# Own PSUM banks for two products of the first down projection, and half of W_out prepared one set earlier

## Chip, cores and metric

The kernel runs on one core of one Trainium2 chip. The metric is the device time of one launch in microseconds (us). Before the change it was 1612.12 us, the median of three runs (1608.09 to 1612.94).

## What is computed

```python
x = attention(q, k, v)              # chunks of 64, 8 heads of 64, 4608 tokens -> 4608 x 512
h = np.maximum(x @ w_in, 0.0)       # up1:   512 -> 2048
y = h * h @ w_out                   # down1: 2048 -> 512
g = y @ w_gate                      # up2:   512 -> 1536, gate and value
a = g * (1 / (1 + exp(-g))) * (y @ w_val)
out = a @ w_out2                    # down2: 1536 -> 512
```

Every large product is exact to float32: a float32 operand is split into a high and a low part, and three matmuls (high by high, weight's low by high, weight's high by low) make one product. The weights come as 64-bit floats that the kernel itself decodes.

## The kernel before, in words

**Tiling.** The 4608 tokens are nine blocks of 512. They are worked on in five sets: `sets[0]` is block 0 alone (a single), `sets[1]` to `sets[4]` are pairs of blocks. For a pair, a 2 x 2 block product is done with seven products in place of eight (Strassen-Winograd); they are numbered 1 to 7, and the weights are kept as a *combo*, a tile `W` with the seven weight combinations, high and low parts. For a product the operands `hi` and `lo` are made by ScalarE (`high`, line 170) and VectorE (`low`, line 173).

**up1.** For each set there are eight jobs, one for each pair of feature blocks (keys 0 to 7); a job is seven products of six matmuls (42 matmuls; the matmuls of every product stand in `three`, lines 551 to 553), in four *quarters*, so that a set has 32 quarters. `beside1` (the function that is called at every quarter `t`) puts other work beside the products: the attention of the next pair, the sums for the next set, and in the last set the preparation of W_out. Keys 0, 3 and 6 of W_in stay in SBUF, the five others move through two slots of the pool `wp` (five slots) and are loaded again by `load_combo` (line 262, `W<-wi`). The products' results leave PSUM as copies on ScalarE (line 641: `r`, `u`) and additions on VectorE (line 627: `g`). The attention of a unit is: scores on PE (406), maximum, subtraction and sums on VectorE, exponential on ScalarE, normalising on POOL (445), a transpose on VectorE (483), a copy on ScalarE (492), four small DMAs `p<-z` on the SP queue (501), and the value products on PE (526).

**W_out's preparation** (class `Prep`, lines 200 to 258). Per block `j` of eight: two raw loads (`raw`, line 115), decoding on ScalarE (142, 143), VectorE (147, 148, 160) and POOL (155), four sums on VectorE (236 to 239), then the high parts on ScalarE and the low parts on VectorE. Blocks 0 to 3 are *resident* (`HELD` = 4): they stay in `wp` slots. Blocks 4 to 7 are `Streamed` (line 269): they are made in two `wp` slots, stored to DRAM (`o`, line 287, two stores each, on POOL's queue) and read back product by product (`ow<-o`, line 1002). All eight are queued in `work` and begun in the last up1 set, set 4, streamed ones first; the raw loads stand on SP's queue, two ahead.

**down1** (class `Down`). For a pair it does products 1, 5, 6, 7, 2, 3, 4, each in four steps of twelve matmuls (48 matmuls a product), each into two PSUM banks, called `acc`. Products 1, 6, 7 and 4 go one after the other onto the same two banks `x`, and the running sums are copied out between them: `kept` (line 1071, ScalarE) takes `r1` after product 1, `u2` after 6, `u3` after 7. Products 5 and 3 go onto `z`, product 2 onto `y`. `put` adds (`add`, line 624, VectorE) and stores the results (1082). A pool of six one-bank buffers (`psb`) serves x, z and y; a buffer of two banks (`psa`) is used by the attention and by up2.

**The order of the work.** Only PE's order is fixed by hand from set 2 on (`tc.manual_schedule` for PE); a scheduler places the instructions on ScalarE, VectorE, POOL and SP, and each of these carries out its own list in that order.

Of the kernel before, what the change touches and what calls it, by code (L numbers as in the profile page):

```python
# [10 lines left out]
F32 = mybir.dt.float32  # L11
# [10 lines left out]
P = 128  # L22
# [7 lines left out]
def attention_mlp_mlp_kernel(  # L30
# [75 lines left out]
    class Raws:  # L106


        def __init__(self, sources, ahead):
            self.sources, self.ahead, self.tiles = list(sources), ahead, []  # L110

        def load(self, n):
# [156 lines left out]
    class Streamed(Prep):  # L269


        stages = {}

        @property
        def w(self):
            k = self.key[1] % 2
            if k not in Streamed.stages:
                w = new_combo().rearrange("p x i c -> p (x i c)")
                Streamed.stages[k] = w.rearrange("p (i x c) -> p x i c", i=7, x=2)
            return Streamed.stages[k]  # L280

        def put(self, roles):
            i, k = divmod(self.key[1], 2)
            if i not in odram:
                odram[i] = dp.tile([P, 7, 2, 2, half], F32, name=f"o{i}")
            w = self.w.bitcast(F32).rearrange("p x i c -> p i x c")
# [613 lines left out]
    early = up1.loads[len(sets) - 1, keys1[5]]  # L900
    up1.loads[len(sets) - 1, keys1[5]] = up1.loads.pop((len(sets) - 1, keys1[4]))

# [64 lines left out]
    class Down:  # L967

        ORDER = ((1,), (5,), (6,), (7,), (2,), (3,), (4,))
        MAKE, LOAD, WEIGHTS = 2, 5, 3

        def __init__(self):
            self.raw, self.ops, self.w = {}, {}, {}
            self.steps = [
                (n, ps, i)
                for n, bs in enumerate(sets)
                for ps in (self.ORDER if len(bs) == 2 else ((1, 5), (2, 4)))
                for i in range(n1 // 2)  # L980
            ]
            self.loaded = self.made = self.weighted = 0
# [11 lines left out]
        def weights(self, upto):  # L994
            while self.weighted < min(upto, len(self.steps)):
                n, ps, i = self.steps[self.weighted]
                self.weighted += 1
                for p in ps:
                    if 2 * i >= HELD:
                        work.until(lambda: ("o", 2 * i + 1) in stored)  # L1000
                        self.w[n, p, i] = big.tile([P, 2, 2, half], F32R, tag="big", name="ow")
                        nc.sync.dma_start(out=self.w[n, p, i].bitcast(F32), in_=odram[i][:, ROLES[p]])
# [41 lines left out]
        def product(self, ps, n, p, i, first, last=True, on=False):  # L1044
            hi, lo = self.ops.pop((n, p, i))
            ws = []
            for k in range(2):
                j = 2 * i + k
                if j < HELD:
                    work.until(lambda: ("o", j) in combos)  # L1050
                    w = [combos["o", j][:, x, ROLES[p]] for x in range(2)]
                else:
                    w = [self.w[n, p, i][:, k, x] for x in range(2)]
                ws.append(w)
            for e in range(2):
                cols = slice(e * P, (e + 1) * P)
                for k, w in enumerate(ws):
                    three(
                        ps[e],
                        (w[0][:, cols], w[1][:, cols]),  # L1060
                        (hi[:, k, :], lo[:, k, :]),
                        first and i == k == 0,
                        last and 2 * i + k == n1 - 1,
                        on,
                    )
# [7 lines left out]

        def put(self, n, i, j, ps, r):
            for e in range(2):
                if r:
                    add(r[e], ps[e], r[e])
                    o = r[e]
                else:
                    o = one("y")  # L1080
                    (nc.vector.tensor_copy if e and len(sets[n]) == 1 else nc.scalar.copy)(out=o, in_=ps[e])
                nc.sync.dma_start(out=ydram[sets[n][j]][1 - i][:, e, :], in_=o)

        def step(self, s):
            n, ps, i = self.steps[s]
            begins, ends = i == 0, i == n1 // 2 - 1

# [18 lines left out]
            elif begins and p == 2:  # L1106
                self.y = two()
            fresh = p in (1, 5, 2)
            self.product(self.z if p in (5, 3) else self.y if p == 2 else self.x, n, p, i, fresh, True, not fresh)
            if not ends:  # L1110
# [162 lines left out]
    HELD = n1 // 2  # L1273
    stored = set()
    down1, down2 = Down(), Last()
# [24 lines left out]
    def beside1(n, m):  # L1300
        def at_quarter(i):
            t = 4 * m + i
            attention_step(n + 1, t)
            attention_step(n + 2, t - LAST)
            if n + 1 < len(sets):
                if t == 24:
                    x_sums(n + 1)
                if t - LAST in OPS:
                    up1.ops[n + 1].make(*OPS[t - LAST])
            else:  # L1310
                work.step(OUT_STEPS[t])
                if t == 17:
                    load_combo(early)
                if t == LAST - 8:
# [6 lines left out]

    def note(j):
        stored.add(("o", j))
        return
        yield

    OUT_STEPS = [1 if t < 4 else 0 if t < 6 else 3 if t % 3 else 2 for t in range(LAST)]

    attention_step(3, -3)
    with ordered(ET.PE):  # L1330
        for n in range(2, len(sets)):
            if n + 1 == len(sets):
                order = [*range(HELD, n1), *range(HELD)]
                raws = Raws([w_out[j + n1 * t] for j in order for t in range(2)], 2)
                made = {j: (Prep if j < HELD else Streamed)(("o", j), raws, j < HELD, False, by_columns) for j in order}
                for j in order:
                    work.add(made[j].steps())
                    work.add(note(j))
            for m in range(n1):
# [251 lines left out]
```

## Time and profile before

| | |
|---|---|
| median of three runs | 1612.12 us |
| the profiled execution, its own time | 1610.74 us |
| its span, first to last instruction | 1608.9 us |
| PE busy | 1557.7 us (97%) |
| VectorE, ScalarE, POOL busy | 1172.7, 819.0, 160.4 us |
| DMA, mean over the span | 241 GB/s |

The span is 1.8 us shorter than the time of the same execution. PE's share of busy time is high all through, so what can be saved is the time between matmuls, and it is read by stage: set 3 of up1 runs from about 281 to 366 us, set 4 (the last) to about 460, down1 from there to about 813, up2 and down2 after that.

### The profile page before, as it was taken

The page shows a single profiled execution, that of the slowest core. Times are in us where ns is not written, and L with a number is a line of the kernel's source. Part 1 is how long each engine was busy: PE and PEld are TensorE (multiplying, and loading weights), DVE is VectorE, ACT ScalarE, POOL GpSimd, SP SyncE. Part 2 cuts the span into 40 slices and gives each one's busy share as a digit, 9 for nine tenths or more (in the row PEclk, how much of TensorE's full clock was granted, in tenths as well). Part 3 has the DMA queues.
Part 4 walks back from the last instruction along what each step waited for, and adds up shares of the span by engine and source line. Part 5 has one row for each costly group of instructions (what it writes and reads, how often), then busy time and mean ns, then how long its engine had stood idle before and what let it go on. Part 6 is the DMA issues. An engine that isn't in the chain of part 4 may idle for free.

```text
span 1608.9 us, 23565 instructions
## 1 busy us (share of the span) xinstructions
PE 1557.7 (97%) x9216; PEld 1279.8 (80%) x9216; DVE 1172.7 (73%) x1392; ACT 819.0 (51%) x1137; POOL 160.4 (10%) x126
## 2 busy tenths in 40 slices
PE   5999999999889999999999999999999999999998
PEld 4788778888668887888788878888888887888886
DVE  7897555657797888998856667457458986887794
ACT  4777666668664544454454444334335644443441
POOL 3122120303300000011001010000000210000000
PEclk9999999999999999999999999999999999999999
DMA  8566786768986887787654644761666999464342
GB/s 315 198 240 216 262 312 222 266 225 287 419 305 232 310 294 272 269 324 274 213 216 186 230 160 157 248 230 53 239 239 237 401 377 407 159 209 146 103 131 53
DMA packets 143679, 387.41 MB, mean 241 GB/s; under 512 B 48465, under 2 KB 57681, under 8 KB 136273
## 3 DMA queue, kind: packets, MB, share of 16 engines
q1 hardware_dynamic: 123600, 327.19, 57.3%
q10 hardware_dynamic: 14592, 38.80, 6.4%
q0 software_dynamic: 5376, 19.92, 3.6%
q8 instruction: 72, 1.18, 0.3%
q14 instruction: 39, 0.31, 0.1%
HBM read 251.92 MB, written 130.81 MB: 238 GB/s over the span
## 4 chain that ended last, share of the span: by engine, by line
PE 89%; DMA 4%; DVE 4%; issue 2%; ACT 1%; POOL 1%; SPq 0%; POOLq 0%; DVEq 0%; ACTq 0%
PE px L551 11%; PE px L553 11%; PE px L552 11%; PE acc L551 7%; PE acc L552 7%; PE acc L553 7%; PE py L551 6%; PE pz L551 6%; PE pz L553 5%; PE pz L552 5%; PE py L553 5%; PE py L552 5%; PE xps L526 1%; DMA raw<-in_w_out_dram 1%; PE s L406 1%
## 5 line engine op out<-in xcount | busy, mean ns | idle before, releaser
L551 PE MATMUL px<-hi,W 128*128 128x512 f32 x640 | 252.1, 394 | 5.6 <-DMA W<-wi 4.0
L553 PE MATMUL px<-lo,W 128*128 128x512 f32 x640 | 249.7, 390 | 0.0
L552 PE MATMUL px<-hi,W 128*128 128x512 f32 x640 | 249.7, 390 | 0.0
L170 ACT CAST hi<-graw 128x1024 fp32r<-128x1024 f32 x124 | 128.1, 1051 | 136.3 <-PE acc L553 39.9
L155 POOL TENSOR_TENSOR m<-m,raw 128x512 int32<-128x512 int32 x68 | 100.9, 1504 | 953.2 <-ACT raw L143 342.3
L641 ACT COPY u<-px 128x512 f32<-128x512 f32 x160 | 92.7, 580 | 156.8 <-PE px L553 149.0
L551 PEld LDWEIGHTS px<-hi,W 128*128 128x128 f32 x640 | 120.4, 188 | 34.8 <-DMA W<-wi 5.0
L170 ACT CAST hi<-h 128x1024 fp32r<-128x1024 f32 x93 | 95.7, 1053 | 96.8 <-DVE h L1181 14.6
L553 PEld LDWEIGHTS px<-lo,W 128*128 128x128 f32 x640 | 120.4, 188 | 25.5
L552 PEld LDWEIGHTS px<-hi,W 128*128 128x128 f32 x640 | 120.4, 188 | 24.4
L551 PE MATMUL pz<-hi,W 128*128 128x512 f32 x320 | 126.3, 395 | 7.1 <-DVE g L627 6.8
L551 PE MATMUL py<-hi,W 128*128 128x512 f32 x320 | 126.3, 395 | 1.1 <-ACT g L786 1.1
L173 DVE TENSOR_TENSOR lo<-graw,hi 128x1024 fp32r<-128x1024 f32 x88 | 109.1, 1248 | 24.8 <-PE acc L552 12.4
L552 PE MATMUL pz<-hi,W 128*128 128x512 f32 x320 | 125.5, 392 | 0.0
L553 PE MATMUL pz<-lo,W 128*128 128x512 f32 x320 | 125.3, 392 | 0.0
L553 PE MATMUL py<-lo,W 128*128 128x512 f32 x320 | 124.9, 390 | 0.0
L552 PE MATMUL py<-hi,W 128*128 128x512 f32 x320 | 124.8, 390 | 0.0
L793 DVE TENSOR_TENSOR g<-g,sig 128x1024 f32<-128x1024 f32 x54 | 65.8, 1220 | 71.8 <-ACT sig L792 71.6
L173 DVE TENSOR_TENSOR lo<-h,hi 128x1024 fp32r<-128x1024 f32 x93 | 110.3, 1211 | 5.4 <-issue 2.2
L551 PE MATMUL acc<-hi,W 128*128 128x512 f32 x256 | 101.0, 394 | 6.0 <-ACT r L1071 5.1
L552 PE MATMUL acc<-hi,W 128*128 128x512 f32 x256 | 100.3, 392 | 0.5 <-DVE W L173 0.5
L551 PE MATMUL acc<-hi,ow 128*128 128x512 f32 x256 | 99.6, 389 | 0.0
(130 smaller groups left out, 3296.3 us busy)
## 6 DMA issues: line engine op xcount, KB each, us to landing
g<-g ACTq DMA_DIRECT2D x72, 512.0 KB, 5.4
graw<-g SPq DMA_DIRECT2D x72, 512.0 KB, 5.6
ow<-o SPq DMA_DIRECT2D x64, 512.0 KB, 5.0
W<-wv SPq DMA_DIRECT2D x16, 1792.0 KB, 8.2
h<-g SPq DMA_DIRECT2D x54, 512.0 KB, 6.6
h<-h SPq DMA_DIRECT2D x54, 512.0 KB, 5.8
W<-wg SPq DMA_DIRECT2D x12, 1792.0 KB, 8.4
W<-wi SPq DMA_DIRECT2D x9, 1792.0 KB, 11.8
```

What stands on the lines that cost most here:

```text
L155: nc.gpsimd.tensor_tensor(out=mi[t], in0=mi[t], in1=halves(word(raw, 0, I32)), op=ALU.add)
L170: nc.scalar.copy(out=hi, in_=src)
L173: nc.vector.tensor_tensor(out=lo, in0=src, in1=hi, op=ALU.subtract)
L406: nc.tensor.matmul(out=s[c * CH:(c + 1) * CH, j, (n * pairs + a) * CH:(n * pairs + a + 1) * CH], lhsT=qt[part, n, cols], rhs=kk[part, n, c ...
L526: nc.tensor.matmul(out=xps[c][j * CH:(j + 1) * CH, (a * 2 + n) * CH:(a * 2 + n + 1) * CH], lhsT=vt[part, n, h * CH:(h + 1) * CH], rhs=rhs, ...
L551: nc.tensor.matmul(out=ps, lhsT=lh, rhs=rh, start=first, stop=False, skip_group_check=on)
L552: nc.tensor.matmul(out=ps, lhsT=ll, rhs=rh, start=False, stop=False, skip_group_check=on)
L553: nc.tensor.matmul(out=ps, lhsT=lh, rhs=rl, start=False, stop=last, skip_group_check=on)
L641: nc.scalar.copy(out=r, in_=self.x)
L793: nc.vector.tensor_tensor(out=g[j], in0=g[j], in1=s, op=ALU.mult)
```

## The change

Two things, which share no code but the order of the blocks.

*Down1's banks.* Product 7 opens two banks of its own (`x7`, the two-bank buffer of `psa`) rather than going on in `x`, and product 4 goes on in them. The sum `u3` is then product 7's banks plus `u2`, two additions on VectorE (`sum_of`) where ScalarE made two copies; after product 4 `put` adds `u2` (two additions on VectorE) where ScalarE made two copies; product 3's result goes to tiles of its own, since `u2` lives on.

*W_out.* The streamed blocks 4 to 7 begin at quarters -30, -21, -11 and -2, counted from the start of set 4, that is from set 3 on, at fixed quarters. Their parts are made in four tiles `os` of the pool `big`, not in `wp` slots, and each is stored by a DMA on ScalarE's queue a quarter later. The resident blocks follow at fixed quarters of set 4. Raw loads stand on POOL's queue, six quarters ahead for streamed blocks, four or five for resident ones. The key order of set 4 becomes 0, 3, 1, 2, 6, 4, 5, 7, with the reloads of keys 4, 5 and 7 tied to the jobs of 3, 1 and 2. The single of down1 takes its feature blocks in the order 2, 3, 0, 1 (the streamed ones first). `make(3)` brings one operand's split forward to quarter 2 of each set.

```diff
         def load(self, n):
             while n > 0 and self.sources:
                 raw = big.tile([P, BLOCK], I64, tag="big", name="raw")
-                nc.sync.dma_start(out=raw, in_=self.sources.pop(0))
+                self.queue.dma_start(out=raw, in_=self.sources.pop(0))
...
     class Streamed(Prep):
-        def put(self, roles):
...
-            nc.gpsimd.dma_start(out=odram[i][:, roles, k], in_=w[:, roles])
-        def l(self):
-            super().l()
-            self.put(slice(0, 3))
-        def n(self):
-            super().n()
-            self.put(slice(3, 7))
+        def stage(self, first, src):
+            w, n = big.tile([P, 2, 2, half], F32R, tag="big", name="os"), src.shape[1]
+            parts_of(src, w[:, :n, 0, :], w[:, :n, 1, :])
             i, k = divmod(self.key[1], 2)
             if i not in odram:
                 odram[i] = dp.tile([P, 7, 2, 2, half], F32, name=f"o{i}")
+            self.put = lambda: nc.scalar.dma_start(out=odram[i][:, first:first + n, k], in_=w.bitcast(F32)[:, :n])
+        def t(self):
+            self.stage(0, self.direct()[:, 0:2, :])
+        def u(self):
+            self.stage(2, self.direct()[:, 2:3, :])
+        def v(self):
+            self.stage(3, self.s[:, 0:2, :])
+        def w(self):
+            self.stage(5, self.s[:, 2:4, :])
...
-    order1[-1] = [keys1[m] for m in (6, 3, 7, 5, 0, 4, 2, 1)]
+    order1[-1] = [keys1[m] for m in (0, 3, 1, 2, 6, 4, 5, 7)]
...
+    for m, after in ((3, 4), (1, 5), (2, 7)):
+        up1.loads[len(sets) - 1, keys1[m]] = keys1[after]
+    up1.loads.pop((len(sets) - 1, keys1[4]))
...
+        SINGLE = (2, 3, 0, 1)
...
+            elif begins and p == 7:
+                x = banks2("x7")
+                self.x7 = [x[:, e, :] for e in range(2)]
-            fresh = p in (1, 5, 2)
+            fresh = p in (1, 5, 2, 7)
+            ps = {5: self.z, 3: self.z, 2: self.y, 7: self.x7, 4: self.x7}.get(p, self.x)
...
             elif p == 7:
-                self.put(n, 1, 1, self.z, self.kept(self.x))
+                self.put(n, 1, 1, self.z, self.sum_of(self.x7, self.u2, "u3"))
             elif p == 2:
                 self.put(n, 0, 0, self.y, self.r1)
             elif p == 3:
-                self.put(n, 0, 1, self.z, self.u2)
+                self.put(n, 0, 1, self.z, self.u2, [one("y"), one("y")])
             elif p == 4:
-                self.put(n, 1, 0, self.x, None)
+                self.put(n, 1, 0, self.x7, self.u2)
...
+            if t == 2:
+                up1.ops[n].make(3)
...
-    OUT_STEPS = [1 if t < 4 else 0 if t < 6 else 3 if t % 3 else 2 for t in range(LAST)]
+    AHEAD, STREAMED = 6, (-30, -21, -11, -2)
+    RESIDENT = (
+        (0, 4, 6, 8, 9, 10, 11), (6, 10, 12, 14, 16, 22, 23), (11, 15, 17, 19, 21, 26, 27), (14, 19, 21, 23, 25, 30, 31),
+    )
...
+            raws = Raws([w_out[j + n1 * t] for t in range(2)], 0, nc.gpsimd)
...
+        for x, j in enumerate(streamed):
+            for y, steps in enumerate(("raw", "d1", "d2 i", "j", "t", "put u", "put q", "v", "put w", "put")):
+                at_time(STREAMED[x] + y - (AHEAD if y == 0 else 0), j, steps)
+        for j, when in zip(resident, RESIDENT):
+            for t, steps in zip(when, ("raw", "d1", "d2 i", "j", "q", "h g", "l n")):
+                at_time(t, j, steps)
```

How the built order changes, at the places that the prediction speaks of:

ScalarE in set 3, from one unit's copy `p<-z` to the next one's exponential; `u`, `r` are the copies that free PSUM banks, `g` up1's results. Before:

```order
L492 COPY p<-z 128x1024
L772 ACTIVATE g_3370<-g_3370 128x1024
L773 DMA g_0_152<-g_3370 128x1024
L432 ACTIVATE e<-e 128x1024
L641 COPY u_3491<-px 128x512
L641 COPY r_3503<-px 128x512
L763 ACTIVATE g_3483<-px 128x512
```

With the change:

```order
L488 COPY p<-z 128x1024
L171 CAST os<-m 128x2x256
L637 COPY u_3514<-px 128x512
L428 ACTIVATE e<-e 128x1024
L171 CAST os<-m 128x256
L637 COPY r_3530<-px 128x512
L279 DMA o_3498<-os 128x2x512
L759 ACTIVATE g_3506<-px 128x512
L279 DMA o_3498<-os 128x512
L768 ACTIVATE g_3506<-g_3506 128x1024
```

The casts into `os` and their stores now stand between the attention's steps and the copies that free banks. A streamed block has four such stores, so there are sixteen.

SP's queue, from the second unit's moves in set 3 (`p<-z`, four DMAs a unit) to the first loads of down1. Before:

```order
L501 DMA p<-z 32x512 x6
L262 DMA W<-wi_2295 128x3584
L501 DMA p<-z 32x512 x6
L262 DMA W<-wi_2235 128x3584
L115 DMA raw<-in_w_out_dram 128x512 x8
L262 DMA W<-wi_1610 128x3584
L115 DMA raw<-in_w_out_dram 128x512 x2
L262 DMA W<-wi_1269 128x3584
L115 DMA raw<-in_w_out_dram 128x512 x2
L262 DMA W<-wi_1105 128x3584
```

With the change:

```order
L497 DMA p<-z 32x512 x8
L263 DMA W<-wi_2235 128x3584
L263 DMA W<-wi_1105 128x3584
L263 DMA W<-wi_1269 128x3584
L263 DMA W<-wi_1610 128x3584
L263 DMA W<-wi_2295 128x3584
L263 DMA W<-wi_2235 128x3584
```

The raw loads of W_out are gone from this queue, and there are two reloads of W_in more (eleven in all against nine). On POOL's queue the raw loads stand now between the attention's loads and its normalising:

```order
L116 DMA raw<-in_w_out_dram 128x512 x2
L386 DMA q<-in_q_dram 128x2x512
L386 DMA k<-in_k_dram 128x2x512
L386 DMA q<-in_q_dram 128x2x512
L386 DMA k<-in_k_dram 128x2x512
L116 DMA raw<-in_w_out_dram 128x512 x2
L391 DMA v<-in_v_dram 128x2x512
L441 TENSOR_TENSOR e<-e,rec 128x1024
L156 TENSOR_TENSOR m<-m,raw 128x2x256 x2
```

Before the change POOL had the same `q`, `k`, `v` and `e` rows there with no `raw` and no `m` among them.

## Rows read from the trace of the kernel before

**Rows 1.** The profile page: busy time of the engines
```profile
PE 1557.7 (97%) x9216; PEld 1279.8 (80%) x9216; DVE 1172.7 (73%) x1392; ACT 819.0 (51%) x1137; POOL 160.4 (10%) x126
```
**Rows 2.** Waits of PE: for what, us in total, times, longest
```profile
PE pz L551 <- DVE g L627: 6.8, 2, 6.5
...
PE acc L551 <- ACT r L1071: 5.1, 3, 2.8
PE px L551 <- DMA W<-wi: 4.0, 1, 4.0
...
PE acc L551 <- DVE g L627: 1.0, 1, 1.0
```
**Rows 3.** Stretches: length, busy of each engine, granted clock, DMA share, GB/s
```profile
281.00:366.00 85.00, 85.00 (x783) 69.35 (x783) 47.97 (x58) 54.05 (x82) 12.61 (x11) 1.00 0.72 247
366.00:400.00 34.00, 34.00 (x151) 28.16 (x150) 28.32 (x42) 26.87 (x41) 11.40 (x11) 1.00 0.80 286
400.00:470.00 70.00, 56.82 (x221) 43.49 (x220) 54.79 (x73) 45.92 (x62) 16.09 (x14) 0.90 0.96 372
470.00:530.00 60.00, 60.00 (x266) 49.69 (x266) 51.04 (x50) 26.99 (x31) 3.56 (x2) 1.00 0.75 249
530.00:616.00 86.00, 83.70 (x368) 68.32 (x367) 73.21 (x71) 45.94 (x55) 7.12 (x4) 1.00 0.85 296
616.00:764.00 148.00, 148.00 (x654) 122.49 (x653) 126.41 (x127) 72.86 (x85) 12.39 (x6) 1.00 0.81 289
764.00:772.00 8.00, 5.22 (x17) 3.87 (x16) 6.91 (x8) 3.57 (x5) 0.00 (x0) 0.79 0.60 227
```
**Rows 4.** The chain of waits in set 4: start us, us, what
```profile
403.53 13.84 DMA W<-wi
...
417.43 20.57 DMA raw<-in_w_out_dram
...
441.58 1.76 DVE m L160
...
445.38 0.69 DVE g L627
```
**Rows 5.** Timeline of PE around two waits of set 4
```profile
431.58 0.80 PE L551 MATMUL px<-hi,W 128*128 128x512 f32 x1 [4.04 <-DMA W<-wi]
432.17 0.63 PE L552 MATMUL px<-hi,W 128*128 128x512 f32 x1
432.60 0.63 PE L553 MATMUL px<-lo,W 128*128 128x512 f32 x1
...
446.11 0.80 PE L551 MATMUL pz<-hi,W 128*128 128x512 f32 x1 [6.50 <-DVE g L627]
```
**Rows 6.** Stretch 400 to 430, columns as in rows 3
```profile
400.00:430.00 30.00, 26.41 (x110) 19.88 (x108) 23.48 (x32) 21.12 (x31) 11.01 (x10) 0.99 1.01 414
```
**Rows 7.** Timeline of ScalarE before the second pair's product 7
```profile
612.43 0.83 ACT L170 CAST W<-m 128x768 fp32r<-128x768 f32 x1
613.16 0.58 ACT L1071 COPY r<-acc 128x512 f32<-128x512 f32 x1
```
**Rows 8.** Groups of instructions in down1: busy us, mean ns, idle before
```profile
L1071 ACT COPY r<-acc 128x512 f32<-128x512 f32 x24 | 13.7, 580 | 2.6 <-PE acc L553 2.6
...
L624 DVE TENSOR_TENSOR r<-acc,r 128x512 f32<-128x512 f32 x24 | 16.1, 682 | 0.7 <-PE acc L553 0.7
```
**Rows 9.** DMA issues: form, count, KB each, median us to landing
```profile
W<-wi SPq DMA_DIRECT2D x9, 1792.0 KB, 11.8
...
p<-z SPq DMA_DIRECT2D x48, 64.0 KB, 3.5
```
**Rows 10.** The chain of waits in set 2, around an attention unit's values
```profile
203.76 13.48 DMA p<-z
217.28 1.15 PE xps L526 x60
```
**Rows 11.** Waits of POOL for VectorE: us in total, times, longest
```profile
POOL o L287 <- DVE W L173: 23.9, 7, 6.1
```

More of the change, by code (lines that the diff above doesn't have):

```diff
@@ L106, in attention_mlp_mlp_kernel, with __init__ @@
     class Raws:
-        def __init__(self, sources, ahead):
+        def __init__(self, sources, ahead, queue=None):
             self.sources, self.ahead, self.tiles = list(sources), ahead, []
+            self.queue = queue or nc.sync
         def load(self, n):
@@ L979, in __init__ @@
                 for ps in (self.ORDER if len(bs) == 2 else ((1, 5), (2, 4)))
-                for i in range(n1 // 2)
+                for i in (range(n1 // 2) if len(bs) == 2 else self.SINGLE)
             ]
@@ L1061, in product @@
                         (hi[:, k, :], lo[:, k, :]),
-                        first and i == k == 0,
-                        last and 2 * i + k == n1 - 1,
+                        first and k == 0 and i == first_duo,
+                        last and k == 1 and i == last_duo,
                         on,
@@ L1072, in kept, with sum_of, put @@
             return r
-        def put(self, n, i, j, ps, r):
+        def sum_of(self, ps, r, name):
+            o = [one(name), one(name)]
+            for e in range(2):
+                add(o[e], ps[e], r[e])
+            return o
+        def put(self, n, i, j, ps, r, o=None):
             for e in range(2):
                 if r:
-                    add(r[e], ps[e], r[e])
-                    o = r[e]
-                else:
-                    o = one("y")
-                    (nc.vector.tensor_copy if e and len(sets[n]) == 1 else nc.scalar.copy)(out=o, in_=ps[e])
-                nc.sync.dma_start(out=ydram[sets[n][j]][1 - i][:, e, :], in_=o)
+                    to = r[e] if o is None else o[e]
+                    add(to, ps[e], r[e])
+                else:
+                    to = one("y")
+                    (nc.vector.tensor_copy if e and len(sets[n]) == 1 else nc.scalar.copy)(out=to, in_=ps[e])
+                nc.sync.dma_start(out=ydram[sets[n][j]][1 - i][:, e, :], in_=to)
         def step(self, s):
             n, ps, i = self.steps[s]
-            begins, ends = i == 0, i == n1 // 2 - 1
+            duos = range(n1 // 2) if len(sets[n]) == 2 else self.SINGLE
+            begins, ends = i == duos[0], i == duos[-1]
             def two():
@@ L1320, in beside1, with out_preps, at_time @@
         return at_quarter
[L1322 to L1325, printed above, removed]
-    OUT_STEPS = [1 if t < 4 else 0 if t < 6 else 3 if t % 3 else 2 for t in range(LAST)]
+    AHEAD, STREAMED = 6, (-30, -21, -11, -2)
+    RESIDENT = (
+        (0, 4, 6, 8, 9, 10, 11), (6, 10, 12, 14, 16, 22, 23), (11, 15, 17, 19, 21, 26, 27), (14, 19, 21, 23, 25, 30, 31),
+    )
+    out_steps = {}
+    def out_preps():
+        streamed, resident = list(range(HELD, n1)), list(range(HELD))
+        made = {}
+        for j in range(n1):
+            raws = Raws([w_out[j + n1 * t] for t in range(2)], 0, nc.gpsimd)
+            made[j] = (Prep if j < HELD else Streamed)(("o", j), raws, j < HELD, False, by_columns)
+        def at_time(t, j, steps):
+            out_steps.setdefault(t, []).append((made[j], steps))
+        for x, j in enumerate(streamed):
[4 more added lines that the diff above has]
+                at_time(t, j, steps)
+    out_preps()
     attention_step(3, -3)
@@ L1331, in attention_mlp_mlp_kernel @@
         for n in range(2, len(sets)):
[L1332 to L1338, printed above, removed]
             for m in range(n1):
```

27 lines of the change are left out of this document (8 added, 19 removed).

## The prediction

> **What bounds the kernel now.** I read the page first: PE is busy 97% of the span [rows 1], so only the time between matmuls can be won. Then the waits of PE: the longest in the touched stages are for a VectorE addition (6.5 us), for a reload of W_in (4.0 us) and, three times, for a copy `r` on ScalarE in down1 (5.1 us together) [rows 2]. Then the stretches, to turn waits into time. From 470 to 530 PE runs 266 matmuls in 60 us, 0.2256 us each; at that pace a stretch has room for a known number, and what is missing is lost, idle or slow clock alike [rows 3]:
> - 281 to 366 (most of set 3) and 366 to 400: nothing is lost (151 of 151 in the second).
> - 400 to 470 (the rest of set 4 and the start of down1): 221 of 310, so 89 x 0.2256 = 20.1 us. Of it 13.2 us are idle (70 - 56.82).
> - 530 to 616: 368 of 381, 3.0 us. 764 to 772: 17 of 35.5, 4.2 us. Between them nothing.
>
> Together 27.3 us, the most the change can win here.
>
> The chain of waits says why set 4 loses 20 us: a W_in reload on its way 13.84 us, then a raw load of W_out 20.57 us, then decoding on VectorE, and only behind it the addition `g` that frees PE's bank [rows 4]. Both loads fall where the DMA engines are full (share 1.01 at 414 GB/s [rows 6]). After the two long waits the matmuls start 0.43 us apart, twice the pace: the clock is at its 1.2 GHz level after PE stood still [rows 5]. Preparing all of W_out within set 4 is thus the bound of that stage, through DMA and through VectorE's list.
>
> In down1 the three losses are one pattern. Product 7 goes on in the banks of product 6 and has to wait until ScalarE has copied them; ScalarE comes to that copy only behind its casts, one of them the weights' preparation [rows 7]. The last of them, 2.8 us, also cost a slow clock (0.79 over those 8 us [rows 3]).
>
> **The change, part by part.**
>
> *Own banks for 7 and 4.* Product 7's first matmul no longer waits for any copy of `u2`. Removed: 3.0 + 4.2 = 7.2 us. Added: of ScalarE's six copies of 0.58 us per pair two go, of VectorE four additions of 0.68 us come (two for `u3`, two after product 4, where two more ScalarE copies go) [rows 8]: 2.7 us of VectorE per pair. VectorE is 85% busy in 530 to 616 (73.21 of 86) and would be near 88%. What covers it: PE's list of waits has no row for an operand's low part in down1 [rows 2], so VectorE runs ahead there; and product 3, the first that needs `z` free, comes 48 matmuls = 10.8 us after product 7, against four additions of 0.68 us. If that cover fails, PE waits at product 3 in place of product 7. Bounds: 0 to the old 7.2 us; I take 0.5 us left.
>
> *Half of W_out from set 3 on.* Removed from set 4: half of the decoding, 4 x 1 MB of raw loads, and 5.5 of the 7.3 MB of stores. The reload that was late (1792 KB, 11.8 us to landing [rows 9]) is issued after the jobs of keys 3, 1 and 2, four to five jobs of 42 x 0.2256 = 9.5 us before use. So the 4.0 us wait, the 6.5 us wait and the slow clock behind them should go. What stays: the bank wait at the border to down1 (1.0 us [rows 2]), and some waits behind resident blocks, whose raws are only four or five quarters of 2.4 us ahead, on POOL's queue behind its adds. Lower bound 0 (as in 366 to 400, where VectorE is 83% busy and PE loses nothing [rows 3]), upper the 20.1 us of today; I take 2.5 us, near the lower, because the DMA share falls.
>
> *What set 3 pays.* Three and a half blocks now share set 3 with the attention. ScalarE is 64% and VectorE 56% busy there, the DMA share is 0.72 [rows 3]. DMA is the tightest: 247 GB/s x 85 us = 21.0 MB; add 4.2 MB of raws, 5.5 MB of stores (1.8 MB a block) and one W_in reload of 1.8 MB, less some 2 MB of raws that were loaded from 351 us on: 30.5 MB in 85 us = 359 GB/s, against 414 GB/s when full [rows 6]; by shares 0.72 + 9.5/35.2 = 0.99. The weak link is `p<-z`: 3.5 us to landing as a rule, but 13.5 us once in set 2 with a W_in reload in front, and PE then waited for it [rows 9, 10]; the order leaves five quarters, 11.9 us, between an attention unit's turn and its values. Bounds: 0 (as in 366 to 400) to the rate of 400 to 430, 3.6 us idle in 30, so 10 us in 85 [rows 3, 6]. I take 3 us, nearer to the first, since blocks come at half the density of 366 to 400. A gain is excluded, as set 3 has no idle time now.
>
> By the Trainium skill (DMA: Bandwidth & Descriptors, Specifications) a core has about 358 GB/s of HBM. No run here shows that limit: the trace moves 414 GB/s for 30 us, and the measurement decides. By the page set 3's traffic would fill the set to the last microsecond and I would take the 10 us, the second rival below.
>
> *The rest.* `make(3)` earlier, the order of keys and of the single's blocks: no operation more, and the spared waits of `make(3)` are none today (PE has no such row [rows 2]). Two reloads more fall after the last unit's moves. Nothing.
>
> **The sum.** 1610.74 - 27.3 + 0.5 + 2.5 + 3 = 1589.4 against the profiled execution's own time, which is 1.4 us under the median of the runs; so I say **1589 us** for the median, 1.4% faster. About 0.3% (4.8 us) is what a measurement of this kernel can tell from no change.
>
> **Rivals.**
>
> *1. Set 3 starves on DMA.* For it: share 0.99 by the sum above, and `p<-z` was late once already at a lower share. Against: most of the added bytes can wait, only the moves and q, k, v can't. Price: 10 us in place of 3, so 1596; with a slow clock behind two waits of over 2.8 us (as at 764 to 772, 1.4 us each) up to 1600.
>
> *2. The late loads only move.* The resident half keeps its raws behind POOL's adds and casts that need a freed `wp` slot, and the waits of set 4 come back in full: only down1's part is won. 1610.74 - 7.2 + 0.5 = 1604. For it: the wait of 6.5 us came from one block's raw. Against: half the bytes, twice the lead.
>
> *3. Slower: the stores block ScalarE.* Sixteen stores on ScalarE's list wait for VectorE's low parts. On POOL the like waited 23.9 us in 7 cases, 3.4 us each, at no cost [rows 11]. On ScalarE everything behind stands, above all the copies `r` and `u` that free banks: `r` has product 5 to hide in, 6 x 0.2256 = 1.35 us less its own 0.58, so 0.8 us. The change puts a quarter (2.4 us) in front of each store, which leaves 1.0 us of 3.4 and costs 16 x 0.2 = 3 us, inside my set 3 term. It decides if VectorE, with more to do there, falls behind by as much as the quarter gives: at 3 us a store PE loses 16 x 2.2 = 35 us and the time is 1622; the balance of the whole change is at 2.2 us a store (21.5/16 + 0.8). By the Trainium skill (DMA: Bandwidth & Descriptors, Anatomy of one DMA) any wait of a DMA happens on the issuing engine's sequencer before dispatch. The rows agree in kind: POOL shows these waits as its own [rows 11]; how long the ScalarE ones last no run of before shows.
>
> **Chances.** Forecast 0.66 (1583 to 1595), rival 1 0.17, rival 2 0.09, rival 3 0.08. Rivals 1 and 2 are still faster by over 0.3%, save where both meet. So faster 0.86, same 0.07, slower 0.07. The range runs from 1582 (all 27.3 us won, and the runs 1.4 us apart) to 1602 (rival 1 and part of rival 2); some 2 in 10 stay outside.
>
> **What would show it.** In the profile after: no wait of PE for ScalarE's `r` in down1, and 616 to 764 like today; in set 4 no wait for `W<-wi` and none of over 2 us for `g`, the granted clock 1.00 from 400 to 470's counterpart on; in set 3 the DMA share over 0.9 and PE idle under 5 us, with waits for `p<-z` or `u`, if any. I am wrong if set 3 loses more than 10 us, if ScalarE shows waits of over 2 us at the stores, or if down1 gains a wait at product 3.

## The result, and the profile after

The changed kernel takes 1589.51 us (median of 4 runs, 1588.57 to 1591.54) against 1610.46 us for the kernel before on the same chip (4 runs, 1608.09 to 1612.94): a ratio of 0.987, 95% interval 0.985 to 0.989, so 1.3% faster. Its profiled execution took 1589.62 us, with a span of 1587.8 us.

PE is busy for 8.9 us less, and the waits of [rows 2] have made room for others. The page and PE's waits, with the kernel after (columns as in [rows 1, 2]; the longer waits of the first 50 us, which both kernels have, are left out):

```profile
PE 1548.8 (98%) x9216; PEld 1275.9 (80%) x9216; DVE 1178.8 (74%) x1416; ACT 811.6 (51%) x1129; POOL 167.1 (11%) x134
```
```profile
...
PE xps L522 <- issue: 3.2, 2, 2.4
PE px L547 <- ACT r L637: 3.1, 2, 2.3
...
PE xps L522 <- DMA p<-z: 1.0, 1, 1.0
...
```

Every row of [rows 2] is gone, the two of 6.5 and 4.0 us in set 4 and those of down1. From 460 to 815 us PE waits for nothing. What is new lies in set 3: the values `xps` and the copy `r`. The wait for `p<-z` is none of it: it lies in set 2, at 216.72 us, and the kernel before has the same one (0.97 us at 217.28). The stretches say the same in time (columns and stretches as in [rows 3]):

```profile
281.00:366.00 85.00, 78.40 (x749) 62.83 (x748) 65.64 (x90) 59.71 (x96) 22.89 (x22) 1.00 0.89 323
366.00:400.00 34.00, 34.00 (x152) 28.15 (x151) 27.43 (x38) 26.09 (x41) 13.87 (x14) 1.00 0.99 370
400.00:470.00 70.00, 70.00 (x309) 57.53 (x308) 48.87 (x60) 45.76 (x60) 5.16 (x4) 1.00 0.92 333
...
530.00:616.00 86.00, 86.00 (x381) 71.23 (x380) 75.75 (x80) 41.95 (x48) 7.12 (x4) 1.00 0.78 267
...
764.00:772.00 8.00, 8.00 (x37) 6.61 (x36) 8.00 (x9) 3.60 (x5) 0.00 (x0) 1.00 0.75 248
```

From 400 to 470 PE now runs 309 matmuls where it ran 221, without idle time and at the full clock (1.00, before 0.90). In set 3, from 281 to 366, it stands idle for 85 - 78.40 = 6.6 us, where it had no idle time. To see each stage by itself I take the n-th 512-column matmul of both timelines (6528 in each) and subtract the starts. The change against before, and the prediction's terms:

| stage (starts in the kernel before) | predicted, us | measured, us |
|---|---|---|
| set 3 and the start of set 4 (282.6 to 408.3) | +3 | +7.57 |
| set 4 and its border (408.3 to 486.1) | -20.1 + 2.5 = -17.6 | -19.46 |
| down1 (486.1 to 783.9) | -7.2 + 0.5 = -6.7 | -7.65 |
| everything else | 0 | -1.31 |
| sum | -21.3 | -20.85 |

The sum is right and the largest new cost isn't. So the question for the runs: does each half of the change do what the prediction says of it, and what does set 3 pay 7.6 us for?

The timeline of the kernel after shows its two long waits. PE first:

```profile
305.89 0.30 PE L522 MATMUL xps<-p,v 64*64 64x64 f32 x3 [2.40 <-issue]
...
313.86 0.50 PE L547 MATMUL px<-hi,W 128*128 128x512 f32 x1 [2.35 <-ACT r L637]
```

VectorE in front of the first:

```profile
295.92 0.41 DVE L237 TENSOR_TENSOR s<-m 128x256 f32<-128x256 f32 x1
296.25 0.41 DVE L239 TENSOR_TENSOR s<-m 128x256 f32<-128x256 f32 x1
296.59 1.20 DVE L434 TENSOR_REDUCE sums<-e 128x16 f32<-128x1024 f32 x1
297.72 0.40 DVE L174 TENSOR_TENSOR os<-m,os 128x256 fp32r<-128x256 f32 x1
298.05 0.41 DVE L238 TENSOR_TENSOR s<-s,m 128x256 f32<-128x256 f32 x1
...
300.14 1.53 DVE L174 TENSOR_TENSOR os<-s,os 128x512 fp32r<-128x512 f32 x1 [1.06 <-ACT os L171]
301.60 0.68 DVE L623 CUSTOM_DVE_ANT_0 g<-pz,u 128x512 f32<-128x512 f32 x1
302.20 1.23 DVE L479 STREAM_TRANSPOSE z<-e 128x1024 f32<-128x1024 f32 x1
303.36 1.18 DVE L419 TENSOR_REDUCE mx<-s 128x16 f32<-128x1024 f32 x1
304.57 1.23 DVE L425 TENSOR_TENSOR e<-s,mx 128x1024 f32<-128x1024 f32 x1
```

The same place in the kernel before, VectorE and then PE:

```profile
298.40 1.25 DVE L483 STREAM_TRANSPOSE z<-e 128x1024 f32<-128x1024 f32 x1 [2.09 <-POOL e L445]
...
301.15 1.23 DVE L423 TENSOR_REDUCE mx<-s 128x16 f32<-128x1024 f32 x1 [0.43 <-PE s L406]
302.41 1.22 DVE L429 TENSOR_TENSOR e<-s,mx 128x1024 f32<-128x1024 f32 x1
```
```profile
303.96 1.16 PE L526 MATMUL xps<-p,v 64*64 64x64 f32 x64
```

There `z` was long done when the scores came, `mx` waited for the scores, and `e` ended 0.33 us before the values began (302.41 + 1.22 = 303.63, then 303.96). So this chain had at most a third of a microsecond to spare.

ScalarE in front of the second:

```profile
306.79 0.57 ACT L637 COPY u<-px 128x512 f32<-128x512 f32 x1
310.61 0.38 ACTq L279 DMA_DIRECT2D o<-os  x1
311.03 1.20 ACT L538 COPY x<-xps 128x256 f32<-128x256 f32 x4 [3.67 <-DMA g<-g]
312.09 1.24 ACT L143 ACTIVATE m<-raw 128x512 f32<-128x512 f32 x2
313.20 0.61 ACT L637 COPY r<-px 128x512 f32<-128x512 f32 x1
```

From these I took two theories and a rival. **V**: VectorE now has the W_out block's rows (`s`, `os`) between one attention unit's rows, so that its `sums`, POOL's `e` and the transpose `z` are late; `mx` and `e` of the next scores stand behind `z`, and only when `e` has ended (304.57 + 1.23 = 305.80) may the values, which use the same two-bank PSUM buffer, begin (305.89). VectorE's `os` at 300.14 also stood 1.06 us for its high part from ScalarE, which had itself stood 1.11 us at a store (before 298.54). **S**: ScalarE stands at a store, and everything behind it is late, here the copy `r` that frees PE's bank. **D**, the rival: the DMA engines are full, whatever waits for a transfer is late, and the lists don't matter. The two long waits make up 5.1 of the 7.57 us; the other 2.4 us come with three waits of 0.3 to 0.8 us behind them, on which no run was made.

### The profile page after: what moved, and what is told of

Read it like the earlier page. It is cut to its first block, busy times and chain, and to the rows that moved or that the text cites. A ratio compares the mean times of both kernels' runs of the same rounds, so it can differ in the third digit from the quotient of the medians.

```text
span 1587.8 us, 23632 instructions
## 1 busy us (share of the span) xinstructions
PE 1548.8 (98%) x9216; PEld 1275.9 (80%) x9216; DVE 1178.8 (74%) x1416; ACT 811.6 (51%) x1129; POOL 167.1 (11%) x134
## 4 chain that ended last, share of the span: by engine, by line
PE 71%; DVE 3%; DMA 3%; issue 1%; ACT 1%; POOL 1%; SPq 0%; ACTq 0%; POOLq 0%; DVEq 0%
PE px L547 8%; PE px L548 8%; PE px L549 8%; PE acc L548 5%; PE acc L549 5%; PE acc L547 5%; PE pz L547 4%; PE pz L549 4%; PE pz L548 4%; PE py L547 4%; PE py L548 4%; PE py L549 4%; PE x L548 2%; PE x L547 2%; PE x L549 2%; DMA raw<-in_w_out_dram 2%
## 5 line engine op out<-in xcount | busy, mean ns | idle before, releaser
L156 POOL TENSOR_TENSOR m<-m,raw 128x512 int32<-128x512 int32 x68 | 105.1, 1567 | 932.7 <-DVE m L149 409.6
L1011 DVE TENSOR_TENSOR graw<-graw 128x1024 f32<-128x1024 f32 x68 | 81.9, 1225 | 9.9 <-DMA graw<-g 9.8
L161 DVE SCALAR_TENSOR_TENSOR m<-raw,m 128x512 int32<-128x512 int32 x68 | 71.5, 1068 | 20.8 <-POOL m L156 20.7
L768 ACT ACTIVATE g<-g 128x1024 f32<-128x1024 f32 x72 | 76.4, 1062 | 18.7 <-DVE g L623 15.2
```

Of the source, the lines that this page charges most:

```text
L156: nc.gpsimd.tensor_tensor(out=mi[t], in0=mi[t], in1=halves(word(raw, 0, I32)), op=ALU.add)
L161: nc.vector.scalar_tensor_tensor(out=mi[t], in0=halves(word(raw, 1, I32)), scalar=TOP, in1=mi[t], op0=ALU.bitwise_and, op1=ALU.bitwise_or,)
L768: nc.scalar.activation(out=g, in_=g, func=AF.Square)
L1011: nc.vector.tensor_tensor(out=out, in0=x, in1=y, op=ALU.subtract)
```

## The experiments

All twelve runs in one table. Loss is measured as in the first row of the table above; the longest wait is PE's longest between 281 and 420 us, the clock the granted one of 281 to 366 us. These three columns are read from one profiled execution of each kernel, so they carry no interval.

| kernel | median, us | ratio to before (95%) | loss in set 3, us | longest wait there, us | clock |
|---|---|---|---|---|---|
| the change | 1589.5 | 0.987 (0.985 to 0.989) | 7.6 | 2.4, `xps` | 1.00 |
| own banks alone | 1602.1 | 0.995 (0.994 to 0.996) | 0.0 | 0.7, `r` | 1.00 |
| W_out alone | 1597.9 | 0.992 (0.990 to 0.994) | 8.1 | 2.4, `xps` | 1.00 |
| stores on POOL | 1593.5 | 0.990 (0.988 to 0.992) | 13.6 | 4.6, `u` | 0.98 |
| stores on SP | 1588.0 | 0.986 (0.985 to 0.988) | 6.0 | 1.8, `xps` | 1.00 |
| light stores | 1604.3 | 0.996 (0.995 to 0.997) | 6.4 | 2.4, `xps` | 0.98 |
| more bytes in before | 1628.6 | one run | 5.8 | 2.8, `k` | 0.96 |
| 4 quarters later | 1593.3 | 0.990 (0.988 to 0.992) | 11.2 | 2.0, `u` | 0.98 |
| 8 quarters later | 1593.5 | 0.989 (0.987 to 0.992) | 12.1 | 3.6, `xps` | 0.96 |
| scores before turn | 1595.4 | 0.990 (0.988 to 0.993) | 10.3 | 3.3, `k` | 0.96 |
| sums on POOL | 1594.5 | 0.990 (0.987 to 0.993) | 12.2 | 6.4, `r` | 0.96 |
| scores before turn, stores on SP | 1594.7 | 0.990 (0.987 to 0.992) | 10.8 | 6.3, `k` | 0.96 |
| raws 4 ahead, stores on SP | 1594.4 | 0.990 (0.989 to 0.992) | 11.8 | 2.4, `xps` | 0.96 |

### Each half alone

*Own banks alone*: the kernel before with `x7`, `sum_of` and the changed calls of `put` from the diff.

> The kernel before with nothing but the own banks for products 7 and 4. Theory A (the two parts of the change are independent, and down1's stalls come from the shared banks alone): the three waits of PE for ScalarE's copy r in down1 go, 7 to 8 us, and set 4 keeps its loss of about 20 us: 1610.5 - 7.5 = 1603, 0.5% faster. Theory B (the stalls come from ScalarE being late with weights that are prepared, so that half of their going belongs to W_out's new places): 1606 to 1608, a wait of PE in down1 stays.

*W_out alone*: the changed kernel with

```diff
...
-            fresh = p in (1, 5, 2, 7)
-            ps = {5: self.z, 3: self.z, 2: self.y, 7: self.x7, 4: self.x7}.get(p, self.x)
...
+            fresh = p in (1, 5, 2)
...
-                self.put(n, 1, 1, self.z, self.sum_of(self.x7, self.u2, "u3"))
+                self.put(n, 1, 1, self.z, self.kept(self.x))
...
```

> The changed kernel with products 7 and 4 back in the shared banks. Theory A: 1589.5 + 7.5 = 1597, with the three waits for r back at products 7 and 6 (about 2.8 us the longest). Theory B: 1592 to 1594, one or two of these waits stay away. Set 3 loses as in the changed kernel, 7 to 9 us, and set 4 under 1 us, by either.

Measured: 1602.1 and 1597.9 us, theory A's 1603 and 1597. Stretches of the own banks alone: set 3 untouched, set 4 as bad as in [rows 3], down1 without idle time.

```profile
281.00:366.00 85.00, 85.00 (x784) 69.38 (x783) 47.93 (x59) 54.69 (x83) 12.60 (x11) 1.00 0.71 245
400.00:470.00 70.00, 56.23 (x222) 43.63 (x223) 54.81 (x73) 45.32 (x61) 15.87 (x13) 0.90 0.95 373
...
530.00:616.00 86.00, 86.00 (x381) 71.23 (x380) 76.09 (x76) 45.03 (x52) 7.12 (x4) 1.00 0.84 302
```

With W_out alone PE waits in down1 for one thing, and set 4 is clean (309 matmuls of the change, 311 here):

```profile
PE acc L547 <- ACT r L1070: 5.5, 2, 3.8
```

Matmul by matmul the own banks win 7.65 us in down1, the same as in the whole change. The halves are independent: (1 - 0.9949) + (1 - 0.992) = 1.3%, the whole. One point speaks for B in part: without the banks two of the three waits are left, not three (the longest is 3.8 us, forecast about 2.8).

### Which queue has the stores

```diff
-            self.put = lambda: nc.scalar.dma_start(
+            self.put = lambda: nc.gpsimd.dma_start(
```

(and `nc.sync` for the other).

> The changed kernel with the sixteen stores of the streamed W_out blocks on POOL's queue, not ScalarE's. Theory S (set 3's 8 us are lost because ScalarE stands at a store: for VectorE's low part at 298 us, for an earlier transfer g<-g at 310.6 us, and the copies r behind it free PE's banks late): ScalarE's 3.7 us wait before the attention's x copies goes, PE's 2.5 us wait for r goes, set 3 loses 3 to 5 us and the time is 1585 to 1587. Theory D (the DMA engines are full in set 3, so whatever waits for a transfer is late on any queue): the same bytes move, set 3 loses 7 to 9 us, the time is 1589 to 1591. Theory P (POOL then stands at the store, and the normalising of e behind it is late): set 3 loses more, with PE waiting for p<-z, 1592 or more.

> The same stores on SP's queue. Theory S: ScalarE's waits go as on POOL's queue, 1585 to 1588, unless the attention's moves p<-z, which stand on SP's queue behind the stores, come late: then PE waits for p<-z, and set 3 loses as much as now, 1589 to 1592. Theory D: 1589 to 1591 with waits at the same places as in the changed kernel.

Measured: 1593.5 on POOL, 1588.0 on SP. In both ScalarE's wait of 3.67 us ahead of the copies `x` and PE's wait of 2.35 us for `r` behind it are gone, with the same bytes moved: that is S, and full DMA engines alone don't explain this wait. ScalarE with the stores on SP's queue, at the same place:

```profile
304.45 1.06 ACT L428 ACTIVATE e<-e 128x1024 f32<-128x1024 f32 x1 [0.80 <-DVE e L425]
305.41 0.57 ACT L637 COPY u<-px 128x512 f32<-128x512 f32 x1
305.88 1.20 ACT L538 COPY x<-xps 128x256 f32<-128x256 f32 x4
```

But only 1.6 us of loss go with it, since the next thing is late. On POOL it is worse, as theory P has it, though not by the wait it named: `e` is in time, loads are late. `k` was issued at 302.24 and landed 12.7 us later; the 4.6 us for `u` at 395 us come behind decoding on ScalarE that stands 4.65 us for a raw, which POOL had issued behind a store at 377.66. PE's waits from 281 to 420 us, stores on POOL:

```profile
PE px L547 <- ACT u L637: 4.9, 2, 4.6
PE s L402 <- DMA k<-in_k_dram: 3.2, 1, 3.2
PE xps L522 <- issue: 1.9, 1, 1.9
```

and on SP:

```profile
PE xps L522 <- issue: 1.8, 1, 1.8
PE s L402 <- DMA k<-in_k_dram: 1.1, 1, 1.1
PE px L547 <- ACT r L637: 1.0, 1, 1.0
PE xps L522 <- PE px L549: 1.0, 1, 1.0
```

Whether 1588.0 beats the change's 1589.5 these runs don't tell: the intervals of the two ratios overlap.

### Fewer bytes, more bytes

*Light stores*:

```diff
...
-odram[i][:, first:first + n, k], in_=w.bitcast(F32)[:, :n])
+odram[i][:16, first:first + n, k], in_=w.bitcast(F32)[:16, :n])
...
```

(Left out: the four DMAs in set 2 that fill the rest.)

> The changed kernel, in which each of the sixteen stores moves 16 of its 128 partitions; the rest of the streamed half of W_out is filled in set 2 with other numbers, so that half of down1's weights is not W_out. ScalarE's and VectorE's lists in set 3 stay as they are, and 6.4 MB of stores leave it. Theory D (set 3 loses 7.6 us because the DMA engines are full, and transfers land late): the loss falls under 3 us, the time to 1584 or 1585; ScalarE's wait of 3.7 us behind g<-g goes. Theory V (VectorE's list: the block's rows stand ahead of an attention unit's sums, POOL's e, the transpose z and then mx and e of the next scores come late, and these hold the bank that the values need): the wait of 2.5 us before the values at 305.9 stays, and the loss is 4 to 6 us, 1586 to 1588.

The time as a whole says nothing here: the scheduler issued the four filling transfers at 50.55 us, and PE then waited 14.8 us in an early stage. Set 3 can be read, 15 us later than in the change: from 296 to 381 us the DMA share is 0.80 at 275 GB/s (the change: 0.89 and 323), and the loss falls from 7.6 to 6.4 us. The wait of 2.35 us for `r` is gone, as with the stores on SP (a wait of 1.72 us for `u` at 346.09 is new); the one before the values is the same to 0.01 us:

```profile
317.72 0.39 PE L549 MATMUL px<-lo,W 128*128 128x512 f32 x1
320.50 0.30 PE L522 MATMUL xps<-p,v 64*64 64x64 f32 x3 [2.39 <-issue]
```

So the first wait is no matter of the stores' bytes (V). The second needs both: a store on ScalarE's list, since it goes when the store moves to another queue with all its bytes, and a transfer that lands late, since it goes as well when the store stays and the bytes don't. With light stores ScalarE's store again went out when the `g<-g` before it had landed, but after 9.33 us in place of 10.91, and ScalarE stood 2.02 us before the copies `x` in place of 3.67; D's forecast had this wait gone. D's forecast of the loss, under 3 us, fails; V's 4 to 6 us is closer, and 0.4 us short.

*More bytes in before*: one more store at every third quarter of set 3.

```diff
+            if n + 2 == len(sets) and t % 3 == 0:
+                extra = dp.tile([P, 1792], F32, name=f"extra{t}")
+                nc.sync.dma_start(out=extra, in_=flat(combos[keys1[0]])[:, :1792].bitcast(F32))
```

> The kernel before with eleven more stores of 896 KB (10.1 MB) of a resident W_in combination to DRAM in set 3, one every third quarter, on SP's queue, and nothing else. Theory D: with the DMA engines as full as in the changed kernel set 3 loses 5 us or more, in waits for p<-z, for q, k or v, or for copies behind g<-g. Theory V: set 3 loses under 2 us, since no engine's list has anything new in it but SP's.

This answered nothing. The scheduler, finding no reason to wait, issued the eleven stores between 27 and 41 us, and the 12 us that the start took longer moved everything behind it. Set 3 had no more bytes (223 GB/s from 290 to 375 us) and yet lost 5.8 us, by one late load of `k` (2.8 us) and the slow clock behind it: the load took 15.8 us to land where the same one took 12.0 us in the kernel before. That kernel had only 1.0 us to spare there (issued at 299.06, landed at 311.06, used at 312.08).

### The blocks later

```diff
-    AHEAD, STREAMED = 6, (-30, -21, -11, -2)
+    AHEAD, STREAMED = 6, (-26, -17, -7, 2)
```

(and `(-22, -13, -3, 6)`).

> The changed kernel with the streamed blocks four quarters later (-26, -17, -7, 2). Theory V: the blocks still lie on three of the four attention units, so set 3's loss changes little, 5 to 8 us, but the place changes: the wait before the values of the first unit shrinks. Theory D: the same bytes a little later, 6 to 8 us. Set 4 still loses under 1 us: 1588 to 1590.

> The changed kernel with the streamed blocks at -22, -13, -3 and 6, eight quarters later at the start. Theory V: the first two attention units have VectorE to themselves, their waits go, set 3 loses 3 to 5 us; 1585 to 1587 if set 4 takes the last block without a loss (VectorE is 69% busy there, 41.5 of 60 us). Theory D: set 3 loses 6 to 8 us as before, since raws and stores are as many. Theory E (set 4 can take no more): set 4 loses 2 us or more, with waits for g behind decoding; 1590 or more.

Both medians are 4 us higher, though the intervals overlap the change's at their ends, and here V's forecast falls: the loss doesn't shrink to 3 to 5 us but grows to 11 and 12. D's 6 to 8 us falls with it. What holds of V is the place: with the second table the wait at 305 us is gone and one of 3.65 us stands before the values of the next unit at 319 us, where the first block now lies. And set 4, where 366 to 400 and 400 to 460 have 1.3 and 2.6 us without a matmul, doesn't take the last block for nothing: theory E has the time, though the waits there are for ScalarE's `u` and `r` and not for `g`. In the tables tried, a block costs a wait where it lies across an attention unit, and later places add others, for `u` 3.8 us in four waits from 358 to 447 us.

### Lists and buffers

*Scores before turn*: the transpose `z` goes behind `mx` and `e` on VectorE.

```diff
-        for what in ("out", "turn", "scores", "qk"):
+        for what in ("out", "scores", "turn", "qk"):
```

> The changed kernel with the attention's steps of a quarter in the order values, scores, turn (before: values, turn, scores), so that VectorE has mx and e of the new scores ahead of the transpose z of the unit before. The same instructions in all. Theory V (z waits for POOL's e, and mx and e, which free the bank that the values need, stand behind it): the wait of 2.5 us before the values at 305.9 goes to under 0.5 us; set 3 loses 4 to 6 us in place of 7.6, the time is 1586 to 1588. Theory L (the wait has another cause, a load of v or the moves p<-z): it stays at 2 us or more, and later moves make it longer; 1589 to 1592.

*Sums on POOL*: the four `s` of a streamed block with `nc.gpsimd.tensor_tensor`.

> The changed kernel with the four sums s of each streamed block (4 x 0.41 us on VectorE) on POOL. Theory V: a unit's sums, POOL's e and z come 1 us or more earlier, the wait at 305.9 falls to about 1 us, set 3 loses 5 to 6.5 us, 1587 to 1588.5. Theory P (POOL's list is as tight in its order as VectorE's: e and the loads of q, k, v stand behind the sums and their waits): the wait stays or moves to a load of k or v, 1590 or more.

*Scores before turn, stores on SP*: both edits.

> The new order of the attention's steps and the stores on SP's queue together. By theories V and S each takes away its own wait (2.5 us before the values, 2.5 us for r), so set 3 loses 3 to 5 us and the time is 1584 to 1586.5, the best so far. If the waits replace one another (another unit's copy or load of k then comes last), it is 1587 to 1589, like either alone.

*Raws 4 ahead, stores on SP*: `AHEAD` is 4, and the stores are `nc.sync`'s.

> The changed kernel with its stores on SP's queue and W_out's raws of the streamed blocks four quarters ahead, not six, so that each of these raws holds its buffer of the pool big for less time; the instructions are the same. Theory B (the loads of q, k and v on POOL's queue come late because the buffers of big that they need are held by os tiles until the stores have landed, which POOL shows as waits for o<-os of 2.6 us at 303 us): these waits go, and with them PE's wait for k (1.1 us with the stores on SP's queue), and set 3 loses 3.5 to 5 us in place of 5.8: 1585.5 to 1587.5. Theory P (the order of POOL's list, not buffers, makes k late): PE's wait for k stays at 1 us or more, or the raws now come late for the decoding and VectorE stands behind them: 1588 or more.

The direct test of V goes the way it says, not as far, and not in the time. With scores before turn the wait of 2.40 us before the values is down to 0.97 us (forecast: under 0.5), and set 3 loses 10.3 us (forecast: 4 to 6). V's last link holds in every run: wherever PE waited before the values of these two units, 15 times in eleven kernels, they began 0.10 us after VectorE's `e` had ended. But in this kernel the load of `k` for another unit is late by 3.28 us, and the time is 1595.4. PE there:

```profile
319.20 1.08 PE L402 MATMUL s<-k,q 64*64 64x64 f32 x29 [3.28 <-DMA k<-in_k_dram]
...
321.70 0.63 PE L548 MATMUL py<-hi,W 128*128 128x512 f32 x1
322.13 0.63 PE L549 MATMUL py<-lo,W 128*128 128x512 f32 x1
```

The matmuls behind the wait start 0.43 us apart, and the granted clock is 0.50, the 1.2 GHz level:

```profile
319.20:322.00 2.80, 2.80 (x66) 2.58 (x67) 2.56 (x3) 0.00 (x0) 2.63 (x4) 0.50 1.08 445
322.00:325.00 3.00, 3.00 (x8) 2.32 (x8) 2.96 (x4) 1.23 (x2) 0.61 (x2) 0.50 1.01 418
```

With the stores on SP besides, 0.18 us is left of the change's two waits, and `k` is late by 6.26 us; the loss of 10.8 us is far from both of that run's forecasts. Sums on POOL cut the first wait to 1.1 us, as V says, and raise the one for `r` to 6.4, so that the time is P's.

Why `k` is late shows on POOL and in its landing. POOL's loads in the change, with scores before turn, and with raws 4 ahead and stores on SP:

```profile
303.75 0.74 POOL L386 DMA_DIRECT2D q<-in_q_dram  x1 [2.63 <-DMA o<-os]
305.33 0.72 POOL L386 DMA_DIRECT2D k<-in_k_dram  x1 [0.83 <-ACT p L488]
```
```profile
307.54 0.72 POOL L386 DMA_DIRECT2D k<-in_k_dram  x1 [2.82 <-DMA o<-os]
```
```profile
308.36 0.72 POOL L386 DMA_DIRECT2D k<-in_k_dram  x1 [7.41 <-DMA o<-os]
```

`q`, `k` and `v` take their tiles from the pool `big`, as `os` and `raw` do, and a tile that is stored is free only when the store has landed (2.8 to 13.8 us after its issue, 7.1 in the middle). So the load is issued late, and then it is long on its way: 10.7 us in the change, 11.5, 8.9, and 13.5 with scores before turn and stores on SP. In the change it landed at 305.33 + 10.7 = 316.03, and its scores began at 316.82. Only 0.8 us lay between, *after* the two waits of 2.4 us: whoever takes these waits away comes to the scores before `k` is there. That is a third cause beside V and S, and here the DMA engines' load comes in. It reaches VectorE too. With sums on POOL

```profile
309.97 0.69 DVE L634 CUSTOM_DVE_ANT_0 g<-py,r 128x512 f32<-128x512 f32 x1 [6.27 <-DMA o<-os]
```

stood until the store issued at 297.88 had landed (309.85); the low part `os` behind it ended at 311.26, ScalarE's store waited for that (6.50 us), and so came the 6.42 us for `r`. The edit meant to relieve it, raws 4 ahead, let POOL stand longer, not shorter: theory B has its wait and not its cure. That kernel's wait before the values (2.42 us) was in part such a wait, VectorE's `e` having stood 1.13 us for a store, and it took 1594.4 us. No run gave the stores tiles of their own, so this third cause is read from the traces and not shown by an edit that removes it.

## Why the prediction was right, and where it was not

**Down1, right.** Predicted -7.2 + 0.5, measured -7.65, and the own banks alone give the same. The cover named for the four additions held: VectorE is 88% busy in 530 to 616 (75.75 of 86), the figure forecast, and no wait at product 3 came. The term of 0.5 us for what is left was not needed.

**Set 4, right, with a term too large.** W_out alone shows that the waits for `W<-wi` and `g` and the slow clock go with the W_out half. Of the 2.5 us that I left standing some 0.6 were left (20.1 - 19.46). The wait at the border that I took as staying (1.0 us of [rows 2]) went too, and no resident block made PE wait.

**Set 3, the mis-sized term.** "I take 3 us, nearer to the first, since blocks come at half the density of 366 to 400." It measured 7.57 us, inside the bounds of 0 to 10; PE stood idle for 6.6 us there, where the prediction's sign was under 5. The step that failed is the choice of the resource: I called DMA the tightest and `p<-z` the weak link. The DMA estimate was near (359 GB/s and a share of 0.99 forecast, 323 GB/s and 0.89 from 281 to 366, 370 GB/s and 0.99 from 366 to 400), but taking most of the stores away left the first wait as it was. `p<-z` cost nothing in set 3. I had misread it: of 28 `p<-z` in the kernel before whose landing the trace has, 13 took over 6 us and six over 10, three of these in set 3 (the longest 13.09 us, issued at 300.75) without a wait of PE. The transfer with little to spare was `k`, of which I said only that it can't wait. I had compared busy shares of a whole stage (VectorE 56%) with a stretch without attention, and not asked what a few rows of VectorE do between one unit's `sums` and the next one's `e`, with a single two-bank buffer between them and at most 0.33 us to spare.

**Rival 3, real but small.** ScalarE does stand at stores: before 298.54 (1.11 us), 302.37 (1.78, of it 0.7 for the addition `g`), 311.03 (3.67) and 328.92 (3.24). By the prediction's own words, waits of over 2 us at the stores, that is a sign against it; it happened at two stores of sixteen, one of them made PE wait 2.35 us, and taking the stores to SP wins 1.6 us of loss. The kind of wait was another than priced: at 310.61 VectorE's low part had long been ready (306.31 + 0.68 = 306.99), and the store was issued when the transfer `g<-g` of 299.63 had landed, 10.9 us after its issue. Why the store waits for that one no run settles. As priced, with a store that waits for VectorE's low part, it came in a variant: the 6.50 us of ScalarE with sums on POOL.

**Rivals 1 and 2, out as they were put.** In the change PE waits for no transfer in set 3, and the loss stays under rival 1's 10 us. The DMA load has a part all the same: a late landing in the second wait, and `k` right behind the two. The limit of 358 GB/s that I quoted from the Trainium skill (DMA: Bandwidth & Descriptors, Specifications; the page divides a stack by two cores) showed itself as little as before: from 300 to 311 us the change moved 403 GB/s. (The 10 us that the prediction there calls the second rival are its first.) And the late loads did not move on: set 4 has no wait for them.

**The total** of 1589 against 1589.5 is therefore partly luck. The sum started from the profiled execution; counted from the median of the runs, 1612.12, it is 1590.8, and that median itself came out 1.7 us lower with a fourth run. And errors cancel: +4.6 us in set 3 are offset by 1.9 in set 4, 0.9 in down1, and 1.3 elsewhere, of which 1.0 us lie between 147 and 182 us and 0.8 us in up2. Neither was forecast; the first is missing in either half alone and with scores before turn, and what makes it come and go stays open.

What stays open as well is whether set 3 can be had for less than 6 us. Of nine variants none is clearly faster than the change (the time of light stores says nothing), so none of these edits had it; a pool of its own for the stored tiles was not tried.

## What to carry to other kernels

Work that is moved into a stage with "room" has to be placed against the tightest chain of that stage, row by row on each engine's list, and not against its busy share. Where one wait is taken away and the next thing, a few tenths behind, becomes the wait, look for what they share (here a load whose buffer is freed by stores that land late) before removing a second one. And keep the waits short: the one of 3.28 us for `k` with scores before turn put PE back by some 6 us, since the clock fell behind it.

## What the hardware showed that was not expected

*VectorE and POOL.* VectorE's row `os<-s,os` at 300.14 took 1.53 us, where the same row takes 0.69 as a rule. It ended at 301.67, 0.54 us behind POOL's `e`:

```profile
299.23 1.90 POOL L441 TENSOR_TENSOR e<-e,rec 128x1024 f32<-128x1024 f32 x1 [5.14 <-issue]
```

(299.23 + 1.90 = 301.13). With the stores on SP the decoding row `m<-m` at 308.22 took 2.11 us in place of 0.69 and ended 0.56 us behind POOL's `e`. By the Trainium skill (SBUF — State Buffer, Who interferes with whom) VectorE and GpSimd share one pair of ports, and the one that comes second blocks until the other's instruction is over, where VectorE has two SBUF inputs or one of its two-port modes. The trace agrees: the rows are not slowed in proportion. Of the rows `m<-m` and `os` that VectorE began well before POOL's `e` was over, between 281 and 400 us of these runs, all but three ended 0.54 to 0.56 us behind it (the three 0.28 to 0.29). VectorE's additions with one input in PSUM were not held up beside the same `e` (`g<-pz,u`, 0.68 and 0.69 us). It is a cost of putting W_out's VectorE rows beside the attention that my sum had at nothing; by estimate (1.53 - 0.69) some 0.8 us of the first wait of 2.40 us.

*The clock.* Waits of the same length did not have the same price. In the change the clock stayed at 1.00 behind waits of 2.40 and 2.35 us. With light stores it was 0.59 from 322 to 325 us, after a wait of 2.39 us, and with raws 4 ahead 0.71 for 6 us after one of 2.42:

```profile
306.10:309.00 2.90, 2.90 (x68) 2.54 (x69) 2.90 (x5) 1.46 (x2) 0.64 (x1) 0.71 1.08 441
309.00:312.00 3.00, 3.00 (x11) 2.35 (x11) 0.31 (x2) 1.42 (x5) 2.72 (x3) 0.71 1.01 421
```

So the length of a wait alone doesn't tell its price; what does, no run here shows. It is part of why most variants lose 10 to 14 us: in the change and with stores on SP the granted clock stayed at 1.00 from 281 to 420 us, while every other kernel whose loss is over 10 us spent 3 to 7 us of it at 0.50.
